# Two-level products with w1 and w2 on three blocks of 1024 tokens instead of six of 512, all 14 weight forms streamed from HBM

## The chip, the cores and the metric

The kernel runs on one core of one Trainium2 chip. Its time is the device time of one launch in microseconds (us); the median of three runs of the kernel before is 856.4 us (853.79 to 858.35). A profile is one execution of the program, recorded by the hardware profiler. Engines: PE is TensorE (PEld its weight loads, which run beside the matmuls), DVE is VectorE, ACT is ScalarE, POOL is GpSimd, SP is SyncE. ACTq and SPq in the profile are what the sequencers of ACT and SP issue, here DMAs.

## The reference

Retention attention on 8 batches x 8 heads x 576 positions x 64, then a feed-forward product on the 4608 tokens that come out of it. D is the causal decay mask. All is float32.

```python
scores = (q @ k.T) / sqrt(64)              # per batch and head, 576 x 576
x = (scores * D) @ v                       # bridge: x is (8*576, 8*64) = 4608 x 512
h = ((x @ w1) * (x @ w2)) @ w3             # w1, w2: 512 x 1024, w3: 1024 x 1024
out = h @ w_out                            # w_out: 1024 x 512
```

The weights arrive as float64 and are turned into float32 on the chip. w3 and w_out are multiplied with each other once, to w3o (1024 x 512).

## The kernel before, in words

**Products.** A float32 matmul takes two passes on PE, and each pass is a weight load and a matmul in the trace. All large products save multiplications by Strassen's scheme: 7 products of quarter matrices instead of 8, with sums of quarters before and after. Three kinds of stage follow one another on PE:

- `up` (L583): x with w1 and w2 on a block of 192 columns, one level of Strassen. It serves the first batch pair and the short first chunks of the others.
- `up2` (L1003 on, matmuls L1047): x with w1 and w2, two levels of Strassen, on the other three batch pairs. Each half of the 1024 output features has 7 outer products ("forms", numbers 1, 2, 7, 6, 5, 3, 4), and each form has 7 inner products. A step ("slot") is one inner product for w1 and for w2, four passes; an `up2` has 2 halves x 7 forms x 7 slots = 98 slots, 392 passes. A block is 512 tokens, so that a matmul streams N=128 columns.
- `down` (L724): the product w1 part times w2 part with w3o for two tiles of 128 tokens, one level of Strassen, 7 products of 8 passes at N=256. There are 18 of them.

**Weight forms.** A form is a 128 x 1792 tile (896 KB): w1 and w2 quarters (`wA`) and their inner Strassen sums (`wS`). The outer forms 1, 2, 7 and 4 of both halves stay in SBUF in `wA` and `wS`. Forms 6, 5 and 3 are made by `second_sums` (L932, DVE) in the stage s=0, stored in HBM by SP (L946) and fetched again by `fetch` (L972) on ACT's queue: 30 fetches, three per half and `up2`, the three of the second half at slots 26, 33 and 40.

**Evictions.** After each inner product its bank of PSUM (2 KB per partition) is added to a slab in SBUF: by DVE (L1070), by ACT into a ring (L1069) and from there by POOL (L1070), or by an ACT copy (L1077). Product 1 of each form is copied by ACT into a second bank, the `upz` copy (L1075), on which product 2 then accumulates; PE waits for that copy. Form 7 ("wide") goes to two targets at once. At the end of a half, quarters of w1 and w2 parts are multiplied (L1103, POOL or DVE). The `upz` bank holds two tiles in turn.

**Attention** runs between these. A unit is one chunk of 128 positions of two batches, 12 units in the three later batch pairs. For a unit, q and k come as "blocks" (`load_blocks`, L221): 16 DMAs of 32 KB each for q and 16 for k, all on SP. POOL scales q (`scale_blocks`, L231), DVE transposes both (`front_blocks`, L239). k and v also come as whole tiles on ACT's queue (`load`, L140, 512 KB each), and POOL scales v (L253). Then PE makes scores (L282), DVE masks them (L285), PE makes x (`pv`, L324 and L351), ACT copies x (L364) and adds to the running state (L309), and DVE makes the Strassen sums of x (`seven`, L996; `outer_sums`, L1006).

**Order.** The order of the instructions of each engine is written out by hand: an engine does its instructions strictly in program order, DMA issues included. `beside`, `aside`, `within` and `at_slot` are lists of small functions that are called between the products of a `down`, an `up` or an `up2`. From the first block of 512 tokens on, the program is, per block s = 0 to 5: unit, `down`, unit, `down` with the second unit's x inside, `up2`. DVE transposes of a next unit and its loads lie in the `up2`. Two `down`s stand at the end. In the built program DMAs signal their end on 8 semaphores that SP and ACT share in turn; a DMA that gets a semaphore whose last DMA has not landed waits for that landing, and its engine with it.

**Memory.** `room` has three tiles: `ab` (slab), `sums` (Strassen sums, ring) and `xT` (x and its sums).

```python
# up2, one slot (before):
a, b = weights(h, j, pr), token_form(j)[:, RHS[pr]]
z = Z[:, k % 2]
...
for w in range(2):
    nc.tensor.matmul(ps[:, w, :], a[:, w, :], b, start=(pr in (1, 5) and w == 0), stop=True,
                     skip_group_check=True)
```

Of the kernel before, what the change touches and what calls it, by code (L numbers as in the profile page):

```python
# [42 lines left out]
def kernel(  # L43
# [42 lines left out]
    wp = ctx.enter_context(tc.tile_pool(name="wp", bufs=1))  # L86
    hold = ctx.enter_context(tc.tile_pool(name="hold", bufs=1))
    room = {nm: hold.tile([P, n], F32, tag=nm, name=nm) for nm, n in (("ab", 6144), ("sums", 3456), ("xT", 4608))}

    def part_of(nm, at, *dims):  # L90

        n = 1
        for d in dims:
            n *= d
        names = [f"d{k}" for k in range(len(dims))]
        return room[nm][:, at:at + n].rearrange(f"p ({' '.join(names)}) -> p {' '.join(names)}",
                                                **dict(zip(names[1:], dims[1:])))
# [46 lines left out]
    dq = room["sums"][:H, :S]  # L144
# [40 lines left out]
    wA = [wp.tile([P, 2, 2, KD // 2, CV], F32, tag=f"wA{h}", name="wA") for h in halves]  # L185
    wS = [wp.tile([P, 3, 2, 2, 2, P], F32, tag=f"wS{h}", name="wS") for h in halves]

    def A(fp, nm):

        h, m = divmod(fp, 2)  # L190
        if nm in ("S1", "S2", "S4"):
            return wS[h][:, ("S1", "S2", "S4").index(nm), m]
        r, f = {"A11": (0, 0), "A12": (1, 0), "A21": (0, 1), "S3": (0, 1), "A22": (1, 1)}[nm]
        return wA[h][:, r, :, :, m * QC + f * P:m * QC + f * P + P]
# [14 lines left out]
    def load_blocks(g, nm):  # L209

        t = pools["ld"].tile([P, 2 * NP, P // BL, BL], F32, tag="ld_q", name="bl_" + nm)
        for u, g1 in enumerate((2 * NC, 3 * NC) if g == "two" else (g,)):
            i, c = divmod(g1, NC)
            n = sizes[c] // BL
            src = {"k": k, "q": q}[nm][2 * i:2 * i + 2].rearrange("b (p a) s d -> a (b p) s d", a=2)
            for a in range(2):
                for f in range(D // BL):
                    part = (a * (D // BL) + f) * BL
                    for m in range(n):
                        s0 = starts[c] + m * BL  # L220
                        nc.sync.dma_start(t[part:part + BL, :, u * n + m, :],  # L221
                                          src[a, :, s0:s0 + BL, f * BL:(f + 1) * BL].rearrange("m r x -> r m x"))
        live["bl_" + nm, g] = t
# [104 lines left out]
    def pv(g):  # L328
# [26 lines left out]
        def evict():  # L355
# [5 lines left out]
            if i and c:  # L361
                x = live["tk"][:, (c - 1) % 2]
# [277 lines left out]
    def tokens(m, t):  # L640
# [6 lines left out]
        else:  # L647
            n, b = divmod(t, 2)
            return [live["slab"][h][:, :, n, :, b, :] for h in range(2)]
        return [x[:, h * NP:(h + 1) * NP].rearrange("p (m f) s -> p m f s", m=2) for h in range(2)]  # L650

    def rows(m, t):

        if m >= len(small):
            n, b = divmod(t, 2)
            i, half = divmod(m - len(small), 2)
            return [(0, P, (2 * (i + 1) + b) * S + starts[1 + 2 * half + n])]
# [52 lines left out]
    def down(x, y, then=None, last=False, within=None, hold=False):  # L710
# [9 lines left out]

        def product(nm, A, B, on=None):
# [22 lines left out]
        nc.scalar.copy(ot[:, 0, 0], ps[1])  # L744
        product(7, "S3", "T3")
        product(2, "A12", "B21", on=1)
        nc.vector.tensor_tensor(out=a["S4"], in0=a["A12"], in1=a["S2"], op=ALU.subtract)
        product(6, "S2", "T2")
        plus(6, C12, C11)
        if within:  # L750
            within()
# [4 lines left out]
        plus(5, C22, C21)  # L756
        product(4, "A22", "-T4")
        plus(4, C21, C21)
        put(*y, 1)
        if last:  # L760
            put(*x, 0, slice(0, 1))
        product(3, "S4", "B22", on=5)
# [6 lines left out]
        if hold:  # L769
            keep_stores.clear()  # L770

# [104 lines left out]
    live["w3o"] = w3op.tile([P, KF, DM], F32, tag="w3o", name="w3o")  # L876
    todo = [(0, 1, 2), (0, 0, 3), (0, 1, 3)] + [(0, 2, fp) for fp in range(NQ - 1)]
    while multiplied[0] < KF:
# [8 lines left out]
        if ready or not todo:  # L887
# [6 lines left out]
            evict()  # L894
    w3_part.close()
# [13 lines left out]
    dram = ctx.enter_context(tc.tile_pool(name="dram", bufs=1, space=bass.MemoryType.DRAM))  # L909
# [3 lines left out]
    def quarter(h, m, c):  # L913
        return wA[h][:, :, :, c, m * QC:(m + 1) * QC], wS[h][:, :, m, :, c, :]

    def pieces(t):
        n = 4 * QC
        return (t[:, :n].rearrange("p (r j x) -> p r j x", r=2, j=2),
                t[:, n:].rearrange("p (s j x) -> p s j x", s=3, j=2))

    def form_tile(h, j):
        t = F_pool.tile([P, 7 * QC], F32, tag=f"F{j}", name="form")
        live["F", h, j] = t
        return t

    def second_sums(h):

        todo = []

        def tt(out, in0, in1, op=ALU.subtract):  # L930
            for k in range(2):
                todo.append(lambda k=k: nc.vector.tensor_tensor(out=out()[k], in0=in0()[k], in1=in1()[k], op=op))  # L932

        def q(m, c):
            return lambda: quarter(h, m, c)

        def f(j):
            return lambda: pieces(live["F", h, j])

        def new_form(j):  # L940
            todo.append(lambda: form_tile(h, j) and None)

        def keep(j):
            def go():
                t = live["kept", h, j] = dram.tile([P, 7 * QC], F32, tag=f"F{h}{j}", name="kept")
                nc.sync.dma_start(t, live["F", h, j])  # L946
            todo.append(go)

        def ready(*parts):
            fns = [todo.pop(0) for _ in range(len(todo))]  # L950
            if len(fns) == 2:
                return fns
            return [lambda: (fns[0](), fns[1]()) and None, lambda: (fns[2](), fns[3]()) and None]

        tt(q(1, 0), q(0, 0), q(1, 0))
        groups = {"S3": ready()}
        new_form(6)
        tt(f(6), q(1, 1), q(1, 0))
        keep(6)
        groups["S2"] = ready()  # L960
        new_form(5)
        tt(f(5), f(6), q(0, 0), ALU.add)
        keep(5)
        groups["S1"] = ready()
        new_form(3)
        tt(f(3), q(0, 1), f(6))
        keep(3)
        groups["S4"] = ready()
        return groups

    def fetch(h, j):
        nc.scalar.dma_start(form_tile(h, j), live["kept", h, j])  # L972

    def weights(h, j, product):
# [3 lines left out]
        if j in (1, 2, 7, 4):  # L978
            a, b = quarter(h, *{1: (0, 0), 2: (0, 1), 7: (1, 0), 4: (1, 1)}[j])
        else:  # L980
            a, b = pieces(live["F", h, j])
# [4 lines left out]
    live["tk"] = part_of("xT", 1024, 2, 2, 7, P)  # L986
    TT = part_of("sums", 0, 3, 7, P)
    ring = part_of("sums", 2688, 3, 2, P)
    slab = room["ab"].rearrange("p (w q l s) -> p w q l s", w=3, q=4, l=4)
# [3 lines left out]
    def seven(x, engine=nc.vector):  # L993

        def tt(out, in0, in1, op=ALU.subtract):
            return lambda: engine.tensor_tensor(out=out, in0=in0, in1=in1, op=op)  # L996

        return [tt(x[:, :, 3], x[:, :, 2], x[:, :, 3]),
                tt(x[:, :, 4], x[:, :, 3], x[:, :, 0], ALU.add),
                tt(x[:, :, 5:7], x[:, :, 1:3], x[:, :, 4].unsqueeze(2).to_broadcast([P, 2, 2, P]))]  # L1000
# [26 lines left out]
    def up2(side):  # L1027

        Z = new("upz", [P, 2, 2, P], "z")
# [6 lines left out]
        def one(slot, k, pos):  # L1036
            h, j, pr = k // 7, ORDER[k % 7], INNER[pos]
            a, b = weights(h, j, pr), token_form(j)[:, RHS[pr]]
            z = Z[:, k % 2]
            if pr == 1:  # L1040
                begun_at.setdefault(k, [None, None])[0] = new("up", [P, 2, P])
            elif pr == 5:
                begun_at.setdefault(k, [None, None])[1] = new("up", [P, 2, P])
# [14 lines left out]
            def spread(t):  # L1058
                return t.unsqueeze(2).to_broadcast([P, 2, 2, P]) if wide else t
# [35 lines left out]
            for fn in side.get(slot, ()):  # L1095
                fn()
# [68 lines left out]
    for u in two:  # L1165
# [16 lines left out]
    beside.append(lambda: front_blocks("two", "q"))  # L1182
    beside.append(lambda: front_blocks("two", "k"))
# [4 lines left out]
    score_two()  # L1188
    down((1, 0), (1, 1))
    load_blocks(first + 1, "q")  # L1190
    load_blocks(first + 1, "k")
    pv_two()
    load(first + 1, "v", nc.scalar)
    list(strassen_tokens(1, 0))
    down((0, 2), (1, 2))
    scale_blocks(first + 1)
    scale(first + 1, "v")
    sums = {h: second_sums(h) for h in halves}
    up(1, 0, 0)
    aside.extend([lambda: None, lambda: front_blocks(first + 1, "q"), lambda: None,  # L1200
                  lambda: front_blocks(first + 1, "k")])
    up(1, 0, 1)
    load_blocks(first + 2, "q")
    load_blocks(first + 2, "k")
    aside.extend(sums[0]["S3"] + sums[0]["S2"] + sums[0]["S1"] + sums[0]["S4"])
    up(1, 0, 2)
    aside.append(lambda: scale_blocks(first + 2))
    ahead((3, 0), (3, 1), 1)
    up(1, 0, 3)
    while aside:  # L1210
        aside.pop(0)()
    acc_part.close()
    pools["banks"] = ctx.enter_context(tc.tile_pool(name="banks", bufs=1, space=PSUM, reuse_waits="tile"))
    free.extend(f"b{k}" for k in range(6))

    blocks2 = 2 * (NB2 - 1)
    for s in range(blocks2):
        i, c = 1 + s // 2, 1 + 2 * (s % 2)
        g = i * NC + c
        m = len(small) + s  # L1220
        if s == 0:
            pair = ((3, 0), (3, 1)), ((2, 2), (3, 2))
        else:
            pair = ((m - 1, 2), (m - 1, 3)), ((m - 1, 0), (m - 1, 1))
        score(g)
        pv_state(g)
# [128 lines left out]
```

## Time and profile before

The profiled execution has a span of 856.3 us; the runs of the same program took 853.79, 856.4 and 858.35 us. Busy time by stage, from a table of time windows of the trace (us; clock is the TensorE clock granted, 1.00 is full):

| stretch | what runs | length | PE | DVE | ACT | POOL | clock | DMA share |
|---|---|---|---|---|---|---|---|---|
| 215-353 | first `down`s, `up`, s=0 units | 138.0 | 136.05 | 79.09 | 16.39 | 14.14 | 1.00 | 0.41 |
| 353-397 | `up2` s=0 | 44.0 | 40.77 | 34.67 | 14.61 | 28.45 | 1.00 | 0.58 |
| 397-440 | units and `down`s s=1 | 43.0 | 42.71 | 26.70 | 6.28 | 8.24 | 1.00 | 0.38 |
| 440-482 | `up2` s=1 | 42.0 | 39.57 | 25.53 | 15.02 | 26.75 | 1.00 | 0.60 |
| 525.5-569 | `up2` s=2 | 43.5 | 39.76 | 24.72 | 14.62 | 25.51 | 0.96 | 0.59 |
| 611-654.5 | `up2` s=3 | 43.5 | 40.11 | 25.57 | 14.62 | 25.40 | 0.96 | 0.55 |
| 699.5-743 | `up2` s=4 | 43.5 | 40.78 | 25.88 | 14.61 | 25.47 | 0.96 | 0.62 |
| 784.2-828.1 | `up2` s=5 | 43.9 | 43.82 | 27.48 | 16.16 | 25.44 | 1.00 | 0.20 |
| 828.1-856.3 | last two `down`s | 28.2 | 24.82 | 11.69 | 1.49 | 0.00 | 1.00 | 0.10 |

How to read it: PE's time stands beside the length of the stretch; what is missing is time in which PE had nothing that it could do. A time of PE is modelled from the starts of its matmuls, and a few records can be missing. Waits are inferred: "ACT upz L1075" as a releaser means that PE waited until that instruction of ACT had ended.

### The profile page before, as it was taken

What the parts mean: (1) busy time and instruction counts of PE and PEld (TensorE: products, weight loads), DVE (VectorE), ACT (ScalarE), POOL (GpSimd) and SP (SyncE); (2) the same over time, 40 slices, a digit from 0 to 9 for tenths busy, and PEclk for the clock granted to TensorE, in tenths of its full rate; (3) what the DMA queues carried; (4) which work ended last, traced back from release to release, by engine and by line L of the source; (5) the groups of instructions that cost most, each with busy time, mean ns of one, the idle gap of its engine ahead of it and who ended that gap; (6) DMA issues with size and microseconds to landing.
All of it is one profiled execution on the core that took longest, in us unless ns stands there. A gap on an engine that the chain in (4) does not pass through costs nothing.

```text
span 856.3 us, 17479 instructions
## 1 busy us (share of the span) xinstructions
PE 821.7 (96%) x6825; PEld 743.1 (87%) x6825; DVE 555.3 (65%) x984; ACT 265.5 (31%) x574; POOL 233.4 (27%) x228
## 2 busy tenths in 40 slices
PE   7899999999999999899998999899989989999998
PEld 7899999644988998899898988898989888989997
DVE  4889999991653495597566745565556555675563
ACT  4777556670111101332123213221223122312320
POOL 1100020002004010186027502760276017601640
PEclk8999999999999999999999999999999999999999
DMA  9994454442056156437426763644265646510301
GB/s 193 218 225 119 76 146 126 127 113 44 5 105 114 41 164 111 88 47 262 90 58 169 190 120 80 167 142 88 61 169 158 134 96 161 149 50 26 130 1 49
DMA packets 232177, 98.74 MB, mean 115 GB/s; under 512 B 208408, under 2 KB 218904, under 8 KB 232096
## 3 DMA queue, kind: packets, MB, share of 16 engines
q1 hardware_dynamic: 173184, 48.31, 27.5%
q10 hardware_dynamic: 58912, 49.33, 20.3%
q8 instruction: 53, 0.87, 0.4%
q14 instruction: 28, 0.23, 0.1%
HBM read 82.65 MB, written 14.94 MB: 114 GB/s over the span
## 4 chain that ended last, share of the span: by engine, by line
PE 71%; DMA 9%; DVE 9%; issue 3%; POOL 2%; SPq 2%; ACT 2%; ACTq 1%; DVEq 0%; POOLq 0%
PE po L724 21%; PE up L1047 19%; PE up L583 12%; PE ps L534 6%; DMA ld_v<-in_v_dram 4%; PE xps L351 3%; PE upz L1047 3%; DMA bl_q<-in_q_dram 3%; PE sc L282 2%; DVE ab L1070 2%; SPq L221 2%; PE st L305 2%; POOL bl_q L231 1%; PE xps L324 1%; POOL ld_v L253 1%
## 5 line engine op out<-in xcount | busy, mean ns | idle before, releaser
L1070 DVE TENSOR_TENSOR ab<-up,ab 128x256 f32<-128x256 f32 (+1 forms) x324 | 144.3, 470 | 89.6 <-PE up L1047 77.5
L1070 POOL TENSOR_TENSOR ab<-sums,ab 128x256 f32<-128x256 f32 (+1 forms) x120 | 101.8, 864 | 157.5 <-ACT sums L1069 156.8
L724 PE MATMUL po<-w3o,ab 128*128 128x256 f32 x552 | 127.4, 383 | 1.4 <-DVE pm L285 0.9
L724 PEld LDWEIGHTS po<-w3o,ab 128*128 128x128 f32 x552 | 103.0, 190 | 19.0 <-DVE pm L285 2.1
L253 POOL TENSOR_TENSOR ld_v<-ld_v,gk 128x1024 f32<-128x1024 f32 (+1 forms) x18 | 34.7, 1926 | 180.6 <-DMA ld_v<-in_v_dram 180.6
L728 DVE TENSOR_TENSOR ot<-po,ot 128x256 f32<-128x256 f32 x90 | 38.0, 423 | 62.3 <-PE po L724 57.5
L1047 PE MATMUL up<-sums,form 128*128 128x128 f32 x576 | 78.1, 275 | 0.0
L1047 PEld LDWEIGHTS up<-sums,form 128*128 128x128 f32 x576 | 71.0, 192 | 0.0
L583 PE MATMUL up<-xT,wA 128*128 128x192 f32 x384 | 70.2, 327 | 0.0
L588 DVE TENSOR_TENSOR sums<-up,sums 128x384 f32<-128x384 f32 x80 | 44.1, 552 | 38.6 <-PE up L583 37.8
L1047 PE MATMUL up<-xT,wA 128*128 128x128 f32 x432 | 67.3, 285 | 1.9 <-DVE ab L1070 1.5
L724 PE MATMUL po<-wB,forms 128*128 128x256 f32 x288 | 66.7, 381 | 0.0
L583 PEld LDWEIGHTS up<-xT,wA 128*128 128x128 f32 x384 | 63.5, 190 | 0.9 <-issue 0.5
L1047 PE MATMUL up<-xT,wS 128*128 128x128 f32 x432 | 61.8, 276 | 2.4 <-ACT upz L1075 2.4
L1047 PEld LDWEIGHTS up<-xT,wA 128*128 128x128 f32 x432 | 58.9, 199 | 3.8 <-DVE ab L1070 3.5
L724 PEld LDWEIGHTS po<-wB,forms 128*128 128x128 f32 x288 | 54.2, 190 | 7.8 <-PE xps L351 0.5
L1047 PEld LDWEIGHTS up<-xT,wS 128*128 128x128 f32 x432 | 54.8, 192 | 3.0 <-ACT upz L1075 3.0
L285 DVE TENSOR_TENSOR pm<-sc,mask 128x512 f32<-128x512 f32 (+1 forms) x72 | 42.6, 652 | 21.7 <-PE sc L282 21.7
L534 PE MATMUL ps<-wo,w3T 128*128 128x512 f32 x128 | 55.1, 592 | 0.0
L231 POOL TENSOR_TENSOR bl_q<-bl_q,gqs 128x512 f32<-128x512 f32 (+1 forms) x26 | 26.3, 1034 | 104.6 <-DMA bl_q<-in_q_dram 75.2
L1069 ACT COPY sums<-up 128x256 f32<-128x256 f32 x60 | 22.3, 372 | 92.9 <-PE up L1047 92.2
L534 PEld LDWEIGHTS ps<-wo,w3T 128*128 128x128 f32 x128 | 24.3, 190 | 30.1 <-issue 29.7
(136 smaller groups left out, 1395.5 us busy)
## 6 DMA issues: line engine op xcount, KB each, us to landing
form<-kept ACTq DMA_DIRECT2D x30, 896.0 KB, 5.2
raw<-in_moe_w_dram SPq DMA_DIRECT2D x72, 128.0 KB, 3.1
out_dram<-ot ACTq DMA_DIRECT2D x29, 256.0 KB, 2.2
bl_q<-in_q_dram SPq DMA_DIRECT2D x216, 32.0 KB, 2.2
bl_k<-in_k_dram SPq DMA_DIRECT2D x208, 32.0 KB, 2.2
ld_v<-in_v_dram ACTq DMA_DIRECT2D x12, 512.0 KB, 6.5
kept<-form SPq DMA_DIRECT2D x6, 896.0 KB, 4.5
ld_k<-in_k_dram ACTq DMA_DIRECT2D x9, 512.0 KB, 5.1
```

Source lines behind the costliest of these rows:

```text
L231: nc.gpsimd.tensor_tensor(out=part, in0=part, in1=gqs[:, :, n0:n0 + n].unsqueeze(3).to_broadcast([P, NP, n, BL]), op=ALU.mult)
L253: engine.tensor_tensor(out=t, in0=t, in1=gam[:sz, c].unsqueeze(1).unsqueeze(3).to_broadcast([sz, 2, H, D]), op=ALU.mult)
L285: nc.vector.tensor_mul(pm[:sz, b, j, :, :sz], sc[j][:sz, :, :sz], mask[:sz, :sz].unsqueeze(1).to_broadcast([sz, NP, sz]))
L351: nc.tensor.matmul(banks[r][heads[half], b, n, :sz], vs[:sz, b * H + 2 * p + j, :], pm[:sz, b, j, p, :sz], start=(c == 0 and m == 0), stop ...
L534: nc.tensor.matmul(ps, live["w3T", ft][:, g, :], live["wo"][:, g, :], start=(g == 0), stop=(g == KF - 1))
L583: nc.tensor.matmul(ps[:, w, :], a[:, w, r, :], b[:, r, :], start=(new and w == r == 0), stop=(w == r == 1), skip_group_check=True)
L588: nc.vector.tensor_add(c[:, to], ps, c[:, sb])
L724: nc.tensor.matmul(ps[nm], a[A][:, f // 2, f % 2, :], live["W"][B][:, f, :], start=(f == 0 and not on), stop=(f == NP - 1), skip_group_che ...
L728: nc.vector.tensor_add(ot[:, to[0], to[1]], ps[nm], ot[:, sb[0], sb[1]])
L1047: nc.tensor.matmul(ps[:, w, :], a[:, w, :], b, start=(pr in (1, 5) and w == 0), stop=True, skip_group_check=True)
L1069: nc.scalar.copy(got, ps)
L1070: engine.tensor_tensor(out=at(out, l), in0=spread(got), in1=at(old if first and old is not None else out, l), op=ALU.add)
```

## The change

- **Blocks.** The loop over s has three steps instead of six. A block is the 1024 tokens of a batch pair (without its short chunk), `NS = 2 * P`, and an `up2` matmul streams N=256 columns. Evictions, ring copies, `upz` copies and multiplications are half as many on twice the width. `upz` is a single bank-wide tile and no longer two in turn.
- **Weights.** No form stays in SBUF. All 14 are kept in HBM: forms 1, 2, 4 of both halves are stored by SP in the w3 stage, once the raw loads are issued (`keep_quarter`, 12 DMAs); 7, 6, 5, 3 are stored by `second_sums` (8 DMAs). `fetch(n)` brings form n into a ring of four buffers, on SP's queue: 42 fetches, two in the stage between the `up`s, two between the `down`s of s=0, then one at slot 7n+13 of each `up2`, for use 15 slots later.
- **Order.** `second_sums` moves from the s=0 stage and the first `up2` to the first three `down`s and to `up(1,0,0)` and `up(1,0,1)`. The loads of the first units move with it. In s=0, the units stand between the `up`s: unit 0, `up(1,0,1)`, unit 1, `up(1,0,2)`, unit 2, `up(1,0,3)`, `down`, unit 3, `down`, `up2`. In s=1 and 2 four units and four `down`s alternate, each with the next unit's transposes and loads at hooks 3 and 5 and the unit's own x at hook 4. In each of the first two `up2`s two v scalings, the transposes of the next unit, its neighbour's 32 block DMAs (slots 44 to 100), and the fetches stand at fixed slots. The k of the first unit is transposed on PE instead of DVE. Four `down`s stand at the end instead of two.
- **Memory.** `room` is one tile; x's sums, slab, outer sums and two of the fetch buffers lie where `wA`, `wS`, `ab`, `xT` and `sums` were.

```diff
+    def keep_quarter(h, j):
+        for to, fr in zip(pieces(kept(h, j)), quarter(h, j)):
+            nc.sync.dma_start(to, fr)
...
+    whole = [(h, j) for h in halves for j in (1, 2, 4)]
...
             evict()
+            while loaded[0] == len(blocks) and whole:
+                keep_quarter(*whole.pop(0))
...
+    FB = [F_pool.tile([P, 7 * QC], F32, tag=f"F{k}", name="form") for k in range(2)]
+    FB += [part_of(f"F{k}", 0, 7 * QC) for k in (2, 3)]
...
+        def go(j, buf, x, y, op=ALU.subtract):
+            def run():
+                tt(pieces(FB[buf]), x(), y(), op)
+                nc.sync.dma_start(kept(h, j), FB[buf])
+            return run
...
+        return [go(7, 0, q(1), q(7)), go(6, 1, q(4), f(0)), go(5, 0, f(1), q(1), ALU.add), go(3, 1, q(2), f(1))]
-    def fetch(h, j):
-        nc.scalar.dma_start(form_tile(h, j), live["kept", h, j])
+    def fetch(n):
+        nc.sync.dma_start(FB[n % 4], kept(n % 14 // 7, ORDER[n % 7]))
-        if j in (1, 2, 7, 4):
-            a, b = quarter(h, *{1: (0, 0), 2: (0, 1), 7: (1, 0), 4: (1, 1)}[j])
-        else:
-            a, b = pieces(live["F", h, j])
+        a, b = pieces(FB[n % 4])
+    NS = 2 * P
...
-        Z = new("upz", [P, 2, 2, P], "z")
+        z = new("upz", [P, 2, NS], "z")
...
-            z = Z[:, k % 2]
-            a, b = weights(h, j, pr), token_form(j)[:, RHS[pr]]
+            a, b = weights(n0 + k, pr), token_form(j)[:, RHS[pr]]
             if pr == 1:
-                begun_at.setdefault(k, [None, None])[0] = new("up", [P, 2, P])
+                begun_at.setdefault(k, [None, None])[0] = new("up", [P, 2, NS])
...
+    beside.extend([sums[0], lambda: turn_two("q"), lambda: turn_two("k"), sums[1], idle])
     down((0, 0), (0, 1))
...
+    beside.extend([sums[2], idle, idle, idle, sums[3]])
     down((1, 0), (1, 1))
...
+    beside.extend([idle, sums[4], lambda: turn_first("q"), lambda: turn_first("k"), sums[5]])
     down((0, 2), (1, 2))
-    scale_blocks(first + 1)
     scale(first + 1, "v")
-    sums = {h: second_sums(h) for h in halves}
+    aside.extend([idle, idle, sums[6]])
     up(1, 0, 0)
...
+        if s == 0:
+            head(u[0])
+            scale_blocks(u[1])
+            aside.extend([idle, lambda: turn_next(u[0], "q"), lambda: turn_next(u[0], "k")])
+            up(1, 0, 1)
+            tail(u[0])
+            for n in range(2):
+                fetch(n)
+            head(u[1])
...
+        else:
+            todo2 = [((m - 1, t), (m - 1, t + 1)) for t in (4, 6, 0, 2)]
+            for e, g in enumerate(u):
+                head(g)
+                down(*todo2[e], todo2[e + 1] if e < 3 else None, hold=e == 3,
+                     within={3: lambda: turn_next(g, "q"), 4: lambda: tail(g), 5: lambda: turn_next(g, "k")})
...
+            for nm, n0 in (("q", 44), ("k", 58)):
+                for n, go in enumerate(block_loads(nxt + 1, nm)):
+                    at_slot(n0 + n // 2 * 7 + n % 2 * 3, go)
...
+        for n in range(14 if nxt else 10):
+            at_slot(7 * n + (13 if n < 12 else 17 if n == 12 else 12), lambda n=n, s=s: fetch(14 * s + n + 4))
...
-            at_slot(26, lambda: fetch(1, 6))
-            at_slot(33, lambda: fetch(1, 5))
-            at_slot(40, lambda: fetch(1, 3))
...
+    last = [((m, t), (m, t + 1)) for t in (4, 6, 0, 2)]
+    for e in range(4):
+        ot_pool[:] = [F_pool, "F0"] if e % 2 else []
+        down(*last[e], last[e + 1] if e < 3 else None, last=e == 3)
```

## The prediction

> **What bounds the kernel now.** First the page: who is busy, and what chain of work ended last.
>
> ```profile
> PE 821.7 (96%) x6825; PEld 743.1 (87%) x6825; DVE 555.3 (65%) x984; ACT 265.5 (31%) x574; POOL 233.4 (27%) x228
> ...
> PE 71%; DMA 9%; DVE 9%; issue 3%; POOL 2%; SPq 2%; ACT 2%; ACTq 1%; DVEq 0%; POOLq 0%
> PE po L724 21%; PE up L1047 19%; PE up L583 12%; PE ps L534 6%; DMA ld_v<-in_v_dram 4%; PE xps L351 3%; PE upz L1047 3%; DMA bl_q<-in_q_dram 3%; PE sc L282 2%; DVE ab L1070 2%; SPq L221 2%; PE st L305 2%; POOL bl_q L231 1%; PE xps L324 1%;
> ```
>
> PE is the bound: 96% busy, 71% of the chain. So the change can win PE passes, or PE's waits, and nothing else. Second, PE's waits from 215 us on, where all that the change touches on PE lies (waits view, columns: total, times, longest):
>
> ```profile
> PE up L1047 <- ACT upz L1075: 13.4, 7, 3.3
> PE xps L351 <- POOL ld_v L253: 4.0, 3, 1.5
> PE up L1047 <- DVE ab L1070: 1.9, 3, 0.9
> PE po L724 <- DVE pm L285: 0.9, 3, 0.3
> ```
>
> The largest is ACT's `upz` copy. Third, ACT at one of these (timeline, 541 to 549 us):
>
> ```profile
> 542.35 0.37 ACT L1069 COPY sums<-up 128x256 f32<-128x256 f32 x1 [1.94 <-PE up L1047]
> 546.48 0.33 ACTq L972 DMA_DIRECT2D form<-kept  x1
> 546.92 0.37 ACT L1069 COPY sums<-upz 128x256 f32<-128x256 f32 x1 [4.20 <-DMA bl_q<-in_q_dram]
> 547.33 0.36 ACT L1075 COPY upz<-up 128x256 f32<-128x256 f32 x1
> ```
>
> The copy took 0.36 us; it was late because the fetch ahead of it on ACT stood still for some 3.8 us, until a block load of SP had landed: both queues share the semaphores. PE waits there once in each of the middle four `up2`s, 2.35 + 3.24 + 3.31 + 2.02 = 10.9 us of the 13.4. Fourth, the granted clock after two of these waits, and between (time windows, PE alone; then clock, DMA share, GB/s):
>
> ```profile
> 719.00:721.50 2.50, 0.52 (x5) 1.00 0.66 83
> 721.50:725.00 3.50, 3.46 (x17) 0.56 0.95 285
> ...
> 547.70:551.20 3.50, 3.46 (x16) 0.52 0.98 287
> 551.20:569.00 17.80, 17.80 (x161) 1.00 0.46 111
> ```
>
> For 3.5 us the clock is about half. Three `up2`s have this (their clock is 0.96 over 43.5 us, 1.7 us lost each, 5.1 in all).
>
> **Passes (removed and added).** PE starts, by the timeline (start, length, form, matmuls in a row), for N=128 and N=256:
>
> ```profile
> 792.43 2.84 PE L1047 MATMUL up<-sums,form 128*128 128x128 f32 x24
> 795.11 0.61 PE L1047 MATMUL upz<-sums,form 128*128 128x128 f32 x4
> ```
>
> ```profile
> 839.13 7.07 PE L724 MATMUL po<-w3o,ab 128*128 128x256 f32 x32
> 846.03 3.62 PE L724 MATMUL po<-wB,forms 128*128 128x256 f32 x16
> ```
>
> From start to start, N=128 takes 2.68/24 = 0.1117 us a pass, N=256 6.90/32 = 0.2156. The change takes away 6 x 392 = 2352 of the first, 262.7 us, and adds 3 x 392 = 1176 of the second, 253.6: **-9 us**. Twice the width costs 1.93 times. With the N=256 passes from 830.42 to 839.13 (40 in 8.71, 0.2178) it is -6.6; ends -6.6 and -9.1. The weights' fixed part was already hidden, so halving the weight loads brings no more.
>
> **Waits that go.** Fetches leave ACT's queue, so the `upz` waits in mid `up2` go; those at its start (1.2 to 1.4 us of ACT issuing k and v loads) go with the new place of the loads: -13.4. Each slow stretch goes with its wait: -5.1. v's scaling: the load was issued in the same `down` pair that uses it, now a unit (18 us) ahead, against 6.5 us to landing: -4.0. `second_sums` leave the s=0 `up2`, where DVE was late: -1.9. Sum **-24.4**. What stays late next to `upz`: nothing that this view shows; the other waits are 1.9 in total.
>
> A rule of the Trainium skill speaks against the first term: DMA: Bandwidth & Descriptors, section "Issuing engines are not separate DMA queues", says that DMAs of all issuing engines run on the same 16 DMA engines and that another issuer saves only sequencer time. The rows above show ACT's sequencer held, which is just that time, so I keep the term. If instead the transfers were the cause, the 10.9 and 5.1 would stay.
>
> **What is added or moved.**
>
> - k of the first unit: 8 PE transposes; 32 of this kind (L267) kept PE busy for 5.1 us in the first pair, 0.16 each, so 1.3, and 0.6 for the ACT copy (L270) that PE waits for. **+1.9** (0 to 3).
> - `second_sums` in the first three `down`s. 8 sums of about 2.7 us (two DVE operations of 1.2 to 2.1 and 0.95 to 1.3) stand between DVE adds that free PE's banks. In a `down` DVE waits 1.1 to 4.1 us at a time for PE, so most of a sum fits; where it doesn't, I get 1.5 + 1.5 + 0.8 us. The fourth sum overwrites a buffer whose store stands on SP behind 16 block loads, which take 7.7 to 12.9 us; DVE would stand up to 5 us, and behind it the add that PE needs. **+7** (3.8 to 12).
> - Units between the `up`s at s=0. A unit's 32 block loads took SP this long in the stage now (SP timeline):
>
> ```profile
> 321.02 12.86 SPq L221 DMA_DIRECT2D bl_q<-in_q_dram  x16
> 334.32 11.26 SPq L221 DMA_DIRECT2D bl_k<-in_k_dram  x16
> ```
>
>   24.1 us here, beside loads of ACT that share the semaphores; 7.72 + 8.95 = 16.7 at 293 us, undisturbed. An `up` (9.1 us from start to start) and a unit (5.9) take 15.0. So a load round is 1.7 to 9.1 us late, two rounds: 3 to 18. Behind the late loads stand POOL's scaling and DVE's transposes, and behind those evictions. Blocks of the first unit come earlier than needed, so **+7** (2.5 to 18).
> - Four units in a row at s=1, 2: a unit and a `down` are 18.0 us against 16.7 to 24.1, two rounds in each of two blocks that are needed at once (the third is needed only in the `up2`). ACT's k and v loads and its output stores wait for landings in their turn, and behind them the copy that frees a bank for the next `down`. Nearest row: in 397 to 440 us the same work lost 0.3 us of 43. That holds one such round, so I take **+3** (0 to 20).
> - Ends of `up2`: the last multiplications (L1103) are twice as wide, 0.68 us becomes some 1.2 by the adds' rows, two after each other, three ends. **+2.9** (0 to 5).
> - Inside `up2`: fetches come every 7 slots = 6.0 us, land in 3.7 to 7.0, and are needed 15 slots (12.9 us) later. SP needs 9 x 0.49 = 4.4 us of each 6.0 with the block loads between. 14 fetches of 896 KB in 84.5 us are about as dense as six in 44 us, where the DMA share was 0.55 to 0.62. Evictions: doubling the width took 420 to 687 ns on DVE (L1070, 128x256 to 128x512), so DVE's 27 us of 44 become some 45 of 85, and POOL's fall likewise. The single `upz` bank must be evicted within 6.0 us: one ACT copy of 0.59. Covered; **+1** (0 to 8).
> - Stores of all forms (14 of 896 KB, 4.5 us to landing each) lie on SP in the w3 stage, where loads have ended: 0.
>
> Added: 1.9 + 7 + 7 + 3 + 2.9 + 1 = **+22.8**. The total is 856.3 - 9.1 - 24.4 + 22.8 = 845.6, from the span of the profiled execution; it stands 0.1 from the runs' median. I forecast **845 us**.
>
> A second rule, TensorE: Matmul & The Clock Gate, "Part 1: The HAM clock gate", gives an idle window of about 3.4 us ahead of a slow clock; the row above shows it after a wait of 2.02 us. By the rule, new waits of 2 us cost only themselves; by the row each may cost 1.7 more, two or three of them 3 to 5 us.
>
> **Rivals.**
>
> 1. *Slower: SP's block loads become the bound.* The place is s=0 and the `down`s of s=1, 2: ten units follow each other at 15 or 18 us, and SP needs up to 24.1 for each. The gains of 33.5 less the fixed costs (1.9, 2.9) are used up at 28.7 us of new waits. With 6 rounds and some 9 us in the first `down`s that is 3.3 us a round: from about 21.3 us of SP for a unit in the `down`s on, this decides. All at the upper end (12 + 18 + 20 + 8 and the fixed 4.8) give 856.3 - 33.5 + 62.8 = 885; half-way to there from the forecast, 865. For it: 24.1 is in the trace, with the same ACT loads beside. Against: 16.7 is in it too, and all other `down` stages lost under 2 us. It is the rival with the other sign.
> 2. *The waits only move* (about 856): the ones taken out, 24.4, return as others of some 32 us. For it: order by hand with little room between `up`s. Time 852 to 860.
> 3. *The change does more than I count* (about 833): the costs at their low ends, 0 + 3.8 + 2.5 + 0 + 0 + 0 and transposes of 1.9 and ends of 2: 856.3 - 33.5 + 10.2 = 833. For it: PE stood at 42.71 of 43.0 us in 397 to 440, so this order can run without waits.
> 4. *It doesn't do what it says:* forms come late, as all 42 must come in time. Price: landing 15 us instead of 7 is 2 us for each, some 80 us. Against: the longest landing in the trace is 7.0. Chance under 0.02, within rival 1.
>
> **Numbers.** Forecast (838 to 852) 0.44; rival 3 (below 838) 0.22; rival 2 0.13; rival 1 0.21, half of it above 865. The range 829 to 865 leaves out about 0.1 above and 0.04 below. What this measurement can tell from no change is about 0.5%, 4.3 us: faster (below 852) 0.66, same 0.13, slower 0.21.
>
> **What would show it.** In the profile after: the passes of `up2` are 0.216 apart and last 84 to 86 us per block; no wait on ACT's `upz` copies over 1 us; fetches land below 8 us. If PE's waits for DVE, ACT or POOL in s=0 and in the `down`s of s=1, 2 sum to over 15 us with block loads behind them, rival 1 has happened; if passes are at 0.2234 or more, the first term is wrong; if the 10.9 us return in mid `up2`, it was the transfers.

## The result, and the profile after

The changed kernel takes 882.75 us (median; 878.4 to 884.72), the kernel before in the same comparison 857.31: ratio 1.0301, 95% interval 1.026 to 1.0341. It is slower by 3.0%, where 845 us and a range of 829 to 865 were forecast. The profiled execution has a span of 876.7 us, 20.4 more than that of before. It is the fastest of the four (878.4 us), so the two traces account for 20.4 of the 25.4 us between the medians.

Page of the changed kernel, busy times and chain:

```profile
PE 822.5 (94%) x5657; PEld 708.9 (81%) x5657; DVE 543.9 (62%) x791; ACT 247.2 (28%) x444; POOL 218.0 (25%) x147
...
PE 67%; DVE 10%; DMA 10%; SPq 7%; issue 4%; POOL 1%; ACT 1%; DVEq 0%; ACTq 0%; POOLq 0%
```

PE does 1168 recorded matmuls fewer and is as long busy as before; its idle time grew from 34.6 to 54.2 us. SPq, which issues the block loads, went from 2% of the chain to 7%. Then PE's waits from 215 us on (total, times, longest), the view that showed `upz` first in the kernel before:

```profile
PE up L1057 <- DVE room L1080: 12.4, 3, 4.9
PE xps L363 <- POOL ld_v L265: 12.1, 2, 9.4
PE sc L294 <- DVE kT L251: 6.1, 5, 2.4
PE po L743 <- DVE room L702: 5.4, 2, 4.4
PE po L743 <- DVE ot L747: 3.9, 4, 1.9
PE up L596 <- DVE room L601: 2.5, 1, 2.5
PE po L743 <- DVE pm L297: 1.8, 2, 0.9
```

No `upz` copy is left. In its place stand an eviction add at the start of each `up2` (L1080), v's scaling at s=0 (L265), transposes (L251), and others: 45 us against 21. By place, as time lost between starts of matmuls: the first three `down`s some 9 us, the units between the `up`s 18, the starts of the `up2`s 13, the `down`s of s=1 and 2 about 9.5. The clock pays too. These are PE's time windows (busy, clock, DMA share, GB/s) at one of the `up2` starts:

```profile
573.30:578.60 5.30, 0.40 (x2) 0.86 0.42 158
578.60:583.40 4.80, 4.80 (x11) 0.50 0.00 0
```

Summed over the trace from 215 us on, the missing clock (1 minus the granted clock, times the stretch) is 18.8 us against 5.1 before; a part of it lies inside waits, where it costs nothing more.

What the change was to win is there. Matmuls of the last `up2` (start, length, count):

```profile
791.13 5.34 PE L1057 MATMUL up<-room,form 128*128 128x256 f32 x24
796.31 1.03 PE L1057 MATMUL upz<-room,form 128*128 128x256 f32 x4
```

5.18 us for 24 passes are 0.2158 us each, so the passes did get 9 us shorter.

### The profile page after: what moved, and what is told of

It reads as the page before. It is cut to its first block, busy times and chain, and to the rows that moved or that the text cites. A ratio compares the mean times of both kernels' runs of the same rounds, so it can differ in the third digit from the quotient of the medians.

```text
span 876.7 us, 14512 instructions
## 1 busy us (share of the span) xinstructions
PE 822.5 (94%) x5657; PEld 708.9 (81%) x5657; DVE 543.9 (62%) x791; ACT 247.2 (28%) x444; POOL 218.0 (25%) x147
## 4 chain that ended last, share of the span: by engine, by line
PE 67%; DVE 10%; DMA 10%; SPq 7%; issue 4%; POOL 1%; ACT 1%; DVEq 0%; ACTq 0%; POOLq 0%
PE up L1057 23%; PE po L743 16%; PE up L596 10%; SPq L228 7%; PE ps L547 6%; PE upz L1057 4%; DVE room L1080 3%; DMA ld_v<-in_v_dram 3%; PE xps L363 3%; DMA bl_q<-in_q_dram 2%; DMA kept<-form 2%; DMA bl_k<-in_k_dram 1%; PE sc L294 1%; DMA ld_k<-in_k_dram 1%; DVE form L968 1%
## 5 line engine op out<-in xcount | busy, mean ns | idle before, releaser
L1080 DVE TENSOR_TENSOR room<-up,room 128x512 f32<-128x512 f32 (+1 forms) x162 | 125.4, 788 | 109.4 <-PE up L1057 106.3
L596 PE MATMUL up<-room 128*128 128x192 f32 x864 | 144.5, 328 | 5.0 <-DVE room L601 4.2
L596 PEld LDWEIGHTS up<-room 128*128 128x128 f32 x864 | 140.2, 190 | 8.0 <-DVE room L601 5.0
L743 PE MATMUL po<-w3o,room 128*128 128x256 f32 x544 | 128.4, 389 | 11.7 <-DVE room L702 5.4
L1057 PE MATMUL up<-room,form 128*128 128x256 f32 x528 | 128.3, 386 | 7.5 <-DVE room L1080 7.5
L743 PEld LDWEIGHTS po<-w3o,room 128*128 128x128 f32 x544 | 103.2, 193 | 30.8 <-DVE ot L747 5.6
L1057 PE MATMUL up<-room 128*128 128x256 f32 x480 | 117.8, 387 | 4.9 <-DVE room L1080 4.9
L1057 PEld LDWEIGHTS up<-room,form 128*128 128x128 f32 x528 | 102.0, 194 | 22.7 <-DVE room L1080 8.3
L1057 PEld LDWEIGHTS up<-room 128*128 128x128 f32 x480 | 93.5, 195 | 18.5 <-DVE room L1080 5.3
L1080 POOL TENSOR_TENSOR room<-ring,room 128x512 f32<-128x512 f32 (+1 forms) x60 | 83.0, 1399 | 97.5 <-ACT ring L1079 97.5
L265 POOL TENSOR_TENSOR ld_v<-ld_v,gk 128x1024 f32<-128x1024 f32 (+1 forms) x18 | 35.2, 1953 | 157.3 <-DMA ld_v<-in_v_dram 149.5
L601 DVE TENSOR_TENSOR room<-up,room 128x384 f32<-128x384 f32 x80 | 44.1, 553 | 40.2 <-PE up L596 39.8
L363 PE MATMUL xps<-pm,ld_v 128*64 128x128 f32 (+1 forms) x576 | 37.6, 289 | 12.1 <-POOL ld_v L265 12.1
L363 PEld LDWEIGHTS xps<-pm,ld_v 128*64 128x64 f32 (+1 forms) x576 | 33.5, 151 | 16.8 <-POOL ld_v L265 12.7
```

The lines of the kernel that those rows point to most:

```text
L265: engine.tensor_tensor(out=t, in0=t, in1=gam[:sz, c].unsqueeze(1).unsqueeze(3).to_broadcast([sz, 2, H, D]), op=ALU.mult)
L363: nc.tensor.matmul(banks[r][heads[half], b, n, :sz], vs[:sz, b * H + 2 * p + j, :], pm[:sz, b, j, p, :sz], start=(c == 0 and m == 0), stop ...
L596: nc.tensor.matmul(ps[:, w, :], a[:, w, r, :], b[:, r, :], start=(new and w == r == 0), stop=(w == r == 1), skip_group_check=True)
L601: nc.vector.tensor_add(c[:, to], ps, c[:, sb])
L743: nc.tensor.matmul(ps[nm], a[A][:, f // 2, f % 2, :], live["W"][B][:, f, :], start=(f == 0 and not on), stop=(f == NP - 1), skip_group_che ...
L1080: engine.tensor_tensor(out=at(out, l), in0=spread(got), in1=at(old if first and old is not None else out, l), op=ALU.add)
```

## The experiments

Theory A: two separate causes. One is the start of each `up2`, where a DVE add with two inputs in SBUF stands still while POOL reads SBUF. The other is the number of block DMAs on SP: the loads come late where units follow each other closely. Rivals: POOL's results are awaited, DVE has too much to do, or the bytes are the limit and waits only move. All ratios are to the kernel before.

| run | edit | ratio | interval |
|---|---|---|---|
| the change | | 1.0301 | 1.026 to 1.0341 |
| e1 | first form added from PSUM | 1.0134 | 1.0078 to 1.0189 |
| e2 | POOL: v ahead of q at s=0 | 1.0289 | 1.0233 to 1.0345 |
| e3 | 4 block DMAs instead of 16 | 1.0003 | 0.997 to 1.0037 |
| e4 | before, fetches on SP | 0.9836 | 0.9793 to 0.988 |
| e5 | e1 and e3 | 0.9779 | 0.9754 to 0.9803 |
| e6 | e1, stores first | 1.002 | 1.0 to 1.0039 |
| e7 | POOL's work later | 1.0072 | 1.0044 to 1.01 |
| e8 | before, 4 block DMAs | 0.9795 | 0.9772 to 0.9818 |
| e9 | e7, stores first | 1.0024 | 1.0002 to 1.0045 |
| e10 | 8 block DMAs | 1.0029 | 1.0008 to 1.0051 |
| e11 | 16 block DMAs, other rows | 1.0268 | 1.0233 to 1.0303 |
| e12 | e9, two fetches later | 0.9961 | 0.9934 to 0.9987 |

**The start of `up2`.** The changed kernel at s=1, DVE first, then POOL (timeline: start, length):

```profile
570.04 6.04 DVE L1080 TENSOR_TENSOR room<-ring,room 128x512 f32<-128x512 f32 x1 [0.19 <-ACT ring L1079]
576.18 0.69 DVE L1080 TENSOR_TENSOR room<-up,room 128x512 f32<-128x512 f32 x1
```

```profile
568.97 2.63 POOL L265 TENSOR_TENSOR ld_v<-ld_v,gk 64x1024 f32<-64x1024 f32 x1 [11.65 <-DMA ld_v<-in_v_dram]
571.57 3.96 POOL L1017 TENSOR_TENSOR room<-room 128x1792 f32<-128x1792 f32 x1
```

The add takes 6.04 us, its twin 0.69. It ends 0.55 us after POOL's second operation. Its inputs are the ring and the slab, both in SBUF; the next add reads PSUM and SBUF. e1 changes only that:

```diff
-                if by_ring:
+                if by_ring and k:
```

> The changed kernel, but in the first form of an up2 DVE adds straight from PSUM; the ACT copy into the ring ahead of it is left out. Same sums, same POOL work at the same slots. Theory A (the start of up2 is lost to a DVE add with two inputs in SBUF that stands still while POOL reads SBUF): the DVE adds at the start of up2 take 0.7 us instead of 4.2 to 6.0, PE's 12.4 us of waits for L1080 go, and three slow-clock stretches of 1.7 us with them; ratio to before about 1.010 instead of 1.030. Rival B (DVE is late because POOL's sums and v's scaling hold data that it needs, or simply has too much to do there): the waits stay within 3 us of 12.4 and the ratio at 1.03.

DVE in e1 (timeline), and POOL beside it:

```profile
569.35 2.83 DVE L1080 TENSOR_TENSOR room<-up,room 128x512 f32<-128x512 f32 x4
```

```profile
568.06 3.13 POOL L265 TENSOR_TENSOR ld_v<-ld_v,gk 64x1024 f32<-64x1024 f32 x1 [11.34 <-DMA ld_v<-in_v_dram]
571.16 3.98 POOL L1017 TENSOR_TENSOR room<-room 128x1792 f32<-128x1792 f32 x1
```

Four adds take 2.83 us, 0.71 each, while POOL does the same two operations at the same place. PE's wait for L1080 is gone, and the ratio falls by 0.017, some 14 us (17 expected). So neither POOL's results nor DVE's load were the cause. But e1 also leaves out ACT's copy into the ring. e7 keeps that copy and the adds, and moves POOL:

```diff
-            at_slot(8, lambda: scale(nxt - 1, "v"))
+            at_slot(14, lambda: scale(nxt - 1, "v"))
-        at_slot(12, sums2["T4"])
+        at_slot(19, sums2["T4"])
```

> The changed kernel with the first form's ring adds as they were, but POOL's two operations of the start of up2 come later: v's scaling at slot 14 instead of 8, the outer sum T4 at slot 19 instead of 12. Theory A (a DVE add with two SBUF inputs stands still while POOL reads SBUF): with no POOL operation beside the first form DVE's ring adds take 0.7 us again, ratio about 1.013 as with the adds from PSUM. Rival B (the ACT copy into the ring was what cost): PE's waits for L1080 stay near 12 us, ratio 1.03.

The ring adds take 0.68 to 0.69 us in all six places; ratio 1.0072, better than the 1.013 expected. Both ways of parting the two engines cure it. The Trainium skill has this rule in SBUF — State Buffer, section "Who interferes with whom": a DVE instruction with two inputs in SBUF contends with a GpSimd instruction that reads SBUF, and the one that comes second stands still. The rows agree (6.04 against 0.69 us) and go further: the add started ahead of POOL's second operation and stood still through that one too.

The kernel before shows the same standstill in its `up2` of s=0. The same kind of sum of `second_sums` on DVE, both inputs in SBUF, first with POOL idle, then beside POOL's scaling of v (timeline, DVE, then POOL):

```profile
312.07 1.22 DVE L932 TENSOR_TENSOR form<-wA,form 128x1024 f32<-128x1024 f32 x1
...
383.81 2.69 DVE L932 TENSOR_TENSOR form<-wA,form 128x1024 f32<-128x1024 f32 x1
```

```profile
383.52 1.90 POOL L253 TENSOR_TENSOR ld_v<-ld_v,gk 128x1024 f32<-128x1024 f32 x1
```

The second sum ends 1.1 us after POOL's operation, and behind it PE waits 0.9 us for an eviction add.

**The number of block DMAs.** The loads of two successive units at s=1, on SP (timeline), in the changed kernel:

```profile
498.14 12.78 SPq L228 DMA_DIRECT2D bl_q<-in_q_dram  x16
511.02 8.70 SPq L228 DMA_DIRECT2D bl_k<-in_k_dram  x16
519.82 12.14 SPq L228 DMA_DIRECT2D bl_q<-in_q_dram  x16
532.06 7.80 SPq L228 DMA_DIRECT2D bl_k<-in_k_dram  x16
```

Each unit takes 20 to 22 us of SP, where a unit and a `down` take 18. DVE waits for the blocks ahead of its transposes (waits from 230 us on: total, times, longest), and the adds that free PE's banks stand behind them:

```profile
DVE kT L251 <- DMA bl_k<-in_k_dram: 8.8, 3, 3.8
DVE qT L251 <- DMA bl_k<-in_k_dram: 7.0, 3, 4.1
```

e3 keeps bytes and packets and cuts the DMAs to a fourth:

```diff
-                for m in range(n):
-                    s0 = starts[c] + m * BL
+                rows = {"k": k, "q": q}[nm].rearrange("b h s d -> (b h s) d")[g1 * 1024:(g1 + 1) * 1024]
+                engine.dma_start(t[part:part + BL].rearrange("r g m x -> r (g m) x"),
+                                 rows[:, f * BL:(f + 1) * BL].rearrange("(e r) x -> r e x", r=BL))
```

> The changed kernel, but each unit's q and k blocks come by 4 DMAs of 128 KB instead of 16 of 32 KB, the same bytes in the same 128-byte packets, from other rows of q and k (so the values are not those of the reference; the work on them is unchanged). Theory A (what makes block loads late is the number of DMAs on SP and their turn on the shared semaphores): SP's time for a unit falls from 17 to 24 us to about 5, DVE's waits for bl_k (about 17 us) and POOL's order problem at s=0 go, the waits of the downs (about 9.5 us) fall below 3, ratio about 1.005. Rival B (the bytes and packets are the limit): landing of a unit's blocks takes as long as before, ratio 1.025 or more.

SP in e3, for the same part of the program:

```profile
497.45 3.29 SPq L228 DMA_DIRECT2D bl_q<-in_q_dram  x4
506.29 3.49 SPq L228 DMA_DIRECT2D bl_k<-in_k_dram  x4
516.81 2.43 SPq L228 DMA_DIRECT2D bl_q<-in_q_dram  x4
524.86 2.85 SPq L228 DMA_DIRECT2D bl_k<-in_k_dram  x4
```

SP needs 5.3 to 6.8 us for a unit, and 0.030 of the ratio go: 850.8 us of span against 876.7. PE's wait for L1080 stays (12.9 us), as it should if the causes are separate; those for v fall from 12.1 to 3.0, those for kT from 6.1 to 1.0. What the `down`s wait for `ot` stays too (3.9 us in the changed kernel, 4.9 in e3), which theory A did not expect. The transfers are no shorter: the 104448 packets of 128 bytes take 14.9 ns each on average in e3 and 13.5 in the changed kernel. Only the rows differ otherwise, so two runs part rows and number. e10 takes 8 DMAs of the same rows, e11 16:

> The changed kernel, a unit's q and k by 8 DMAs of 64 KB each instead of 16 of 32 KB (4 of 128 KB in e3), the same packets, from other rows (values not those of the reference). Theory A (the number of DMAs counts: SP's 0.49 us each and their turns on the shared semaphores): most of the way from 1.030 to 1.000, ratio 1.003 to 1.012, since 32 x 0.49 = 15.8 us of a unit's 15 to 18 become 7.9. Rival B (what e3 gained came from the rows read, whose addresses lie closer together): with the same rows as e3 the ratio is again 1.000, within 0.003, though there are twice as many DMAs.

> The changed kernel with a unit's q and k in 16 DMAs of 32 KB each, as it has them, but from the same other rows of q and k that e3 and e10 read (values not those of the reference). It takes the number of DMAs out of e3 and leaves the rows. Theory A (the number counts): ratio within 0.005 of the changed kernel's, 1.025 to 1.035, SP's time for a unit 17 to 24 us. Rival B (the rows' addresses made the gain of e3): ratio 1.005 or less.

e11 is at 1.0268, its interval overlapping that of the change: the rows give nothing, or little. e10 is at 1.0029: by itself that lies at the edge of what either theory allowed, but with e11 it says that halving the number gives most of the gain. Whether SP's time for each issue or the turns on shared semaphores weigh more, no run parts. An estimate from the rows above: the fastest round of 16 takes 7.80 us, so at most some 15.6 of a unit's 20 to 22 us are the issues alone.

> The changed kernel with both edits: DVE adds the first form straight from PSUM, and a unit's blocks come by 4 DMAs of other rows of q and k (values not those of the reference). Theory A (two separate causes, one in up2, one in s=0 and the downs): the gains add up, ratio to before 1.000 - 0.017 = 0.983. Rival B (the same slack is freed twice, one cause hides behind the other): 0.993 or more.

e5 has both edits: 0.9779, a little below the sum of the two (0.983). The gains add up, so the causes are separate.

**Does the kernel before have this too?**

> The kernel before with a unit's blocks by 4 DMAs instead of 16, from other rows (values not those of the reference). Theory A (in the kernel before the number of block DMAs costs only where a fetch or a v load meets them): the mid-up2 waits on upz copies and the slow clock go, ratio about 0.98, so that the changed kernel (which gained 0.030 by this) was hit harder by 0.01. Rival B (the kernel before has the same shortage as the changed one): ratio 0.97 or less. Rival C (block loads cost the kernel before nothing): 0.995 or more.

Yes: 0.9795, as theory A had it. Its waits for block loads sat in ACT's fetches: the `upz` waits fell from 13.4 to 2.2 us in e8. So of the 0.030 that the changed kernel gains by fewer DMAs, 0.021 are to be had before, too; it was hit harder by about 0.009. e5 and e8 are the two kernels with neither cause, for in the kernel before the first form's ring adds take 0.42 to 0.43 us and do not stand still: 0.9779/0.9795 = 0.998, which is no difference that these runs can tell. Most of the 9 us of passes is used up there: PE's listed waits are 14.8 us in e5 and 7.3 in e8, and the extra transposes come on top.

**One part of the change alone**, in the kernel before, with the block loads issued later:

```diff
-        nc.scalar.dma_start(form_tile(h, j), live["kept", h, j])
+        nc.sync.dma_start(form_tile(h, j), live["kept", h, j])
...
-            at_slot(32, lambda: front_blocks(nxt, "k"), lambda: load_blocks(nxt + 1, "q"),
-                    lambda: load_blocks(nxt + 1, "k"))
+            at_slot(32, lambda: front_blocks(nxt, "k"))
+            load_slot = 41 if s else 32
...
+        if nxt:
+            at_slot(load_slot, lambda: load_blocks(nxt + 1, "q"), lambda: load_blocks(nxt + 1, "k"))
```

> The kernel before with one part of the change: its 30 fetches are issued on SP instead of ACT, and in the up2 where three fetches of the second half come first the block loads are issued behind the third of them (slot 41 instead of 32), so that no fetch stands behind 32 block loads. Theory A (ACT's sequencer was held by a fetch that waited for a block load's landing): the four mid-up2 waits on upz copies (10.9 us) and the slow clock behind three of them (5.1 us) go, ratio to before about 0.982. Rival B (the transfers themselves were late): the waits come back as waits for form tiles, ratio within 0.5% of 1.

PE's waits in e4:

```profile
PE xps L351 <- POOL ld_v L253: 3.0, 3, 1.2
PE up L1047 <- ACT upz L1075: 2.8, 3, 1.5
```

The `upz` waits fell from 13.4 to 2.8 us, no slow clock is left from 215 us on, and the ratio is 0.9836. No waits for forms came up. ACT's own waits for block loads of q, 14.8 us in four places of the kernel before, are gone in e4, and in e8 too, which leaves the fetches on ACT. So ACT, held by a fetch that waits for a block load, was the cause. e4 changes the queue of the fetches and their order against the loads together; which of the two it needs, no run parts. This version, with six small blocks and the resident forms, beats both kernels.

**Order, in the changed kernel.** e2, e6, e9 and e12 change only what stands ahead of what.

```diff
-                    if nm == "k":
+                    if nm == "k" and s == 0 and g < units[2]:
+                        later.append(after)
+                    elif nm == "k":
                         scale_blocks(after)
...
                 scale(g + 1, "v")
+            while later:
+                scale_blocks(later.pop())
```

That is e2. The next is of e6, e9 and e12, the last of e12 alone; e6 also has e1's edit, e9 and e12 have e7's:

```diff
-    beside.extend([idle, sums[4], lambda: turn_first("q"), lambda: turn_first("k"), sums[5]])
+    beside.extend([idle, sums[4], sums[5], lambda: turn_first("q"), lambda: turn_first("k")])
```

```diff
             tail(u[0])
-            for n in range(2):
-                fetch(n)
...
             tail(u[2])
+            for n in range(2):
+                fetch(n)
```

(In e6, e9 and e12, `load_blocks(first + 1, "q")` of the first `down` also moves behind `sums[1]`.)

> The changed kernel, but at s=0 POOL scales q's blocks of the unit after next behind v of the next unit, not ahead of it. Theory A (PE waits 2.9 and 9.4 us for a v that has long landed, because POOL stands at blocks whose DMAs are late): both waits for L265 shrink below 1.5 us each, slow clock goes with them, ratio to before about 1.013. Rival B (traffic is the limit, waits only move): the waits come back as waits of scores for kT or of adds behind transposes, ratio above 1.024.

A miss of theory A: the 12.1 us for v went, and waits for kT rose from 6.1 to 11.6, for L702 from 5.4 to 8.7. Ratio 1.0289. POOL's order was only where the late blocks showed; here rival B was right.

> The changed kernel with DVE adding straight from PSUM, and with the stores of second_sums ahead of the block loads on SP in the first downs (the loads are issued one or two hooks later). Theory A (DVE waits for stores that stand behind 16 or 32 block loads): DVE's 10 us of waits for kept<-form shrink below 3, PE's waits in the first downs and the first up from about 11 us to under 5; ratio about 1.004 after 1.013. Rival B (SP's loads are the shortage, whatever comes first): the loads land later and the waits for blocks grow by as much, ratio 1.010 or more.

Ratio 1.002. DVE's waits for stores fell from 10.2 us in e1 to 1.4, as A had it, while PE's waits for v rose from 10.8 to 15.7: both theories have a part.

> The changed kernel with POOL's two operations later (slots 14 and 19, as in e7) and the stores of second_sums ahead of the block loads (as in e6), DVE's ring adds as they were. Theory A (separate causes): the 0.011 that the stores gave between e1 and e6 comes on top of e7, ratio about 0.996, and the DVE waits for kept<-form fall from 9 us to under 3. Rival B (the waits go over to the block loads): 1.003 or more.

1.0024 after 1.0072, so about half of the 0.011 came, between what A and B named. DVE's waits for stores fell from 9.0 us in e7 to 0.3, but PE's waits for v are 16.1 us.

> e9 (POOL's two operations later, stores ahead of block loads) and, at s=0, the first two fetches behind the third unit instead of between the first two, where SP otherwise goes on to the block loads of the units that are due. Theory A (a block load takes its turn on a semaphore of a fetch or v load that lands late, and the late blocks hold POOL and so v): SP's 16 loads of q behind the fetches fall from 16 us to under 10, PE's waits of 16.1 us for L265 to under 8, ratio 0.990 to 0.996. Rival B (SP's number of DMAs alone, 32 in a 15 us unit, is too much): the waits stay above 13 us, ratio 1.000 or more.

PE's waits for v fell to 12.7 us, not below 8, and SP's 16 loads of q still take 15.4 to 15.7 us. The ratio is 0.9961: e12 is as fast as the kernel before, within what was called no change, and does not reach e4. Neither bound of the expectation was met; order alone takes 0.034 off the ratio, and SP's 32 issues for a 15 us unit remain.

## Why the prediction was wrong, point by point

In spans the miss is 31.1 us (876.7 against 845.6). Its largest parts are some 13 us inside `up2`, 11 in the units between the `up`s and 6.5 in the `down`s of s=1 and 2.

- **Passes, -9.1:** right. 0.2158 us measured, 0.2156 forecast.
- **Waits that go, -24.4:** the mechanism was right for `upz` (13.4 us to none; e4 confirms the cause). The -4.0 for v was wrong at s=0, where 12.1 us came instead, and right in the later units, where no such wait is left. The 1.9 of `second_sums` is gone from `up2`; the sums' cost is now in the first `down`s. The -5.1 of slow clock was wrong as a net gain: the new waits bring their own. I had written 3 to 5 us for that and left it out of the sum; the missing clock is 18.8 us after against 5.1 before.
- **Inside `up2`, +1 (0 to 8):** this is the step that failed, the one term whose cost lies outside its own range. I compared the busy time of DVE and POOL with the length of an `up2` and called it covered. What counted was that one DVE add with two SBUF inputs meets two POOL operations (one in the last `up2`), in a place where PE waits for its bank: 12.4 us of waits and slow clock behind each, 14 us by e1. The trace before had it to be read: of the three waits that make up the 1.9 us put down to `second_sums`, two (0.9 and 0.5) lie behind DVE sums stretched beside POOL, 2.69 us instead of 1.22 and 1.66 instead of 0.95. The adds of the first form were spared there: the outer sum on POOL came at slot 23, behind that form, and was half as wide (2.09 us).
- **Units between the `up`s, +7 (2.5 to 18):** a term set too low: about 18 us lost, the upper end of its range, by rival 1's mechanism.
- **First `down`s, +7 (3.8 to 12):** about 9 us and two slow stretches. The store behind 16 block loads happened as described; DVE's sums and adds were also stretched there by POOL (a sum of 0.95 us took 1.74).
- **`down`s of s=1 and 2, +3 (0 to 20):** about 9 us. I took the low end from one stretch with a single such load round.
- **Ends of `up2`, +2.9; transposes, +1.9:** both smaller than forecast: one of the three ends lost 1.1 us, the others 0.1, and the 8 transposes took 0.9.
- **Rivals.** Rival 1 (0.21) is what happened in s=0 and the `down`s, with SP at 20 to 22 us a unit, where 21.3 was the point named; the sign named for it, over 15 us of waits there, is seen. Its time of 865 to 885 holds the result, but partly by luck: without the standstill of DVE's adds, which no rival had, the ratio is 1.0134 (e1), some 869 us. Rival 4 did not happen: the fetches landed in 4.3 to 7.5 us, and PE waited for none. The range ended at 865 because the terms were taken near their low ends one by one, though one cause, SP's loads, drives three of them together.

## What to carry to other kernels

Where DVE and POOL work in the same stretch, look at the operands and not at the busy shares: an add with both inputs in SBUF can wait out POOL operations that follow each other, two of them here, and reading one input from PSUM, or moving POOL's work by some slots, took that away. Count the DMAs that one queue has to issue for a period of the loop, with the turns on shared semaphores, before bringing its periods closer together. Several cost terms that hang on one cause are one term with one chance, and their upper ends belong together in the range.

## What the runs showed of the hardware

- A DVE add that waited for POOL's reads did not get its turn between two POOL operations: in the row above it started at 570.04, POOL's first operation ended at 571.60, the second began at 571.57, and the add ended at 576.08. At s=0 it was the same: an add of 5.84 us from 402.45 on, beside POOL operations from 401.94 to 407.75.
- It works the other way, too: POOL's 128x1792 sum took 5.75 us instead of 3.96 where it began (739.23) beside a two-input DVE sum, which ended at 741.14.
- The slow clock does not follow each wait: after 2.06 us of lost time at 263 us PE ran at a granted clock of 0.50, after 2.67 at 309 us it stayed at 1.00.
